# Reading the first batch's tokens in long stretches, fetching weights earlier, and moving the cluster copies to another DMA queue

## The chip, the cores and the metric

The kernel runs on one core of a Trainium2 chip. The metric is device time in microseconds (us) from launch to end; three runs of the kernel before gave 1026.86, 1027.94 and 1029.68, so the median is 1027.94. The profile is of one further execution, which took 1027.27 by the same clock and spans 1025.3 from its first to its last instruction. Sums made from the profile are sums against 1025.3.

## The reference

Two blocks are joined. The first is attention with routing: four batches, eight heads, 768 tokens, 64 numbers per head. Every token's query and key are assigned to the nearest of 16 centroids of the head, and a query only attends to keys of its own cluster. The second is a feed-forward block over all 3072 tokens, with a leaky slope per hidden unit.

```python
q_assign = np.argmax(np.einsum('bhsd,hcd->bhsc', q_n, c_n), axis=-1)
k_assign = np.argmax(np.einsum('bhsd,hcd->bhsc', k_n, c_n), axis=-1)
mask = q_assign[:, :, :, None] == k_assign[:, :, None, :]
scores = np.where(mask, scale * np.matmul(q, k.transpose(0, 1, 3, 2)), -1000000000.0)
attn = softmax(scores)
x = np.matmul(attn, v)             # then (B,H,S,D) -> (B*S, H*D)
h = x @ w_in                       # 512 -> 2048
out = (np.maximum(h, 0.0) + alpha * np.minimum(h, 0.0)) @ w_out   # 2048 -> 512
```

q, k, v and the centroids arrive as float32. The two weight matrices come as 64-bit floats, which the kernel reads as pairs of 32-bit words and turns into float32 itself, 128 by 512 numbers at a time.

## The kernel before, in words

**Steps.** Heads are handled two at a time: a pair `n` is a batch and two heads, 16 pairs in all. A pair's 768 queries are split in two halves of 384. The unit of the schedule is a step `u`: two of the six chunks of 128 keys, for one half of one pair, so three steps make a half. `steps` orders them: all four pairs of batch 0 with half 0 (u = 0 to 11), the same four with half 1 (u = 12 to 23), then batch 1, and so on, 96 steps. As soon as one half of a batch has gone through attention, its feed-forward work is cut into pieces (`ffn_pieces`, lines L611 on) that are spread over the next twelve steps. So u = 0 to 11 have attention alone on TensorE, and every later step has attention and feed-forward work.

**One step.** TensorE computes the scores (L467), for batch 0 it adds a mask product (L477) whose operands are `member` (which cluster a key is in) and `aq` (the same for queries), ScalarE takes the exponential (L488) into `E`, and one step later TensorE weighs the values with `E` (L577). In u = 0 to 11 it also sums the denominators, L570, into one fixed PSUM bank, `first_den`. When a half is done, VectorE turns and inverts the denominators (L583 to L596) and multiplies into `xT` (L604), which the feed-forward block reads (L627).

**Before a pair.** `load` and `load_v` bring q, k and v. For the first batch (`n < NCH`, NCH = 4) tokens lie 128 apart within a partition, so each DMA is cut into pieces of 64 floats, 256 bytes. `prep_features` transposes q and k on TensorE (L325), and ScalarE copies them to `qkT` (L329). `prep_sims` multiplies with the centroids (L352) into PSUM tile `mps`, of which there is one buffer, and `prep_argmax` takes the nearest centroid on VectorE (L360 to L382, seven instructions). `of_heads` (L386, ScalarE) makes the two heads' key masks, and `prep_queries` copies query rows to other partitions with two small DMAs (L427).

**Weights.** `convert` takes one block of 128 by 512 through stages: fetch (DMA, L238), split (VectorE, L241 and L243), scale (ScalarE, L247 and L249), join (VectorE, L253 and L256, then a multiplication on GpSimd, L259). 32 blocks are needed, half of w_in and half of w_out alternating in groups of four. There are five buffers `raw` for the fetched words and three `power`. Fetch is the first stage, so a block's DMA stands two slots ahead of its split in the order of the program; the scale follows four slots after the split and the join two after that.

**Order.** No scheduler is at work: the program's order is written out by hand. Each step has five slots, `later(k, piece)` puts a piece k slots on, and `prep_at` and `load_at` hold what is due at a step. Every engine runs its own instructions in that order. All DMAs but two small ones are issued by SP, in one queue, in program order too: a DMA that waits for a buffer or for an engine holds back those behind it.

```python
load_at.setdefault(max(u - 7, -AHEAD), []).append(
    lambda n=n: n < 2 or (load(n), load_v(n)))
at(u - (3 if n < NCH else 6), FIRST, lambda n=n: prep_sims(n))
at(u - 1, FIRST + h, lambda n=n, half=half, h=h: prep_queries(n, half, h))
converting = 0 if u < 1 else 1 + (u % 3 == 2) if u < UB else 2
```

The last line gives the conversions begun in a step: none at u = 0, 15 by the end of u = 11, two per step from u = 12 (UB) until all 32 are begun.

Of the kernel before, what the change touches and what calls it, by code (L numbers as in the profile page):

```python
# [9 lines left out]
FP32 = mybir.dt.float32  # L10
# [11 lines left out]
def kernel(  # L22
# [67 lines left out]
    def later(slots, piece):  # L90
        due.setdefault(now[0] + slots, []).append(piece)
# [13 lines left out]
    def load(n):  # L105


        b, hp = pairs[n]
        for w, src in enumerate((q, k)):
            raw = inp.tile([P, NJ, 2, D], FP32, name="qk")  # L110
            for h in range(2):
                rows = src[b, 2 * hp + h]
                if n < NCH:
                    nc.sync.dma_start(out=raw[:, :, h, :],
                                      in_=rows.rearrange("(j p) d -> p j d", p=P))
                    continue
                for x in range(D // Q):
                    r = h * D + x * Q
                    nc.sync.dma_start(  # L119
                        out=raw.rearrange("p j h d -> p (j h d)")[r:r + Q, :].rearrange(  # L120
                            "p (t i) -> p t i", i=Q),
                        in_=rows[:, x * Q:(x + 1) * Q].rearrange("(t p) i -> p t i", p=Q))
            raw_qk[n, w] = raw

    def load_v(n):
        b, hp = pairs[n]
        vt = vpool.tile([P, 2, NJ, D], FP32, name="vt")
        nc.sync.dma_start(
            out=vt.rearrange("p h j d -> p (h j) d"),
            in_=v[b, 2 * hp:2 * hp + 2].rearrange("h (j p) d -> p (h j) d", p=P))  # L130
        vts[n] = vt
# [4 lines left out]
    nc.scalar.dma_start(out=alf, in_=moe_alpha.rearrange("(f p) -> f p", p=P))  # L136
    for n in range(2):
        load(n)
        load_v(n)

# [90 lines left out]
    def convert(src, dst):  # L231
        raw = raw_tiles[0]
        raw_tiles.append(raw_tiles.pop(0))
        lo, hi = raw[:, :, 0], raw[:, :, 1]
        power = cvt.tile([P, CW], U32, name="power")

        def fetch():
            nc.sync.dma_start(out=raw.rearrange("p n w -> p (n w)"), in_=src)  # L238

        def split():  # L240
            nc.vector.tensor_scalar(out=power, in0=hi, scalar1=0x7FF00000, scalar2=None,  # L241
                                    op0=ALU.bitwise_and)
            nc.vector.tensor_scalar(out=dst.bitcast(U32), in0=hi, scalar1=0x000FFFFF,  # L243
                                    scalar2=None, op0=ALU.bitwise_and)

        def scale():
            nc.scalar.activation(out=power, in_=power, func=AF.Relu,  # L247
                                 bias=low_exp[:, 0:1], scale=8.0)
            nc.scalar.activation(out=dst, in_=dst.bitcast(U32), func=AF.Identity,  # L249
                                 bias=1.0, scale=2.0 ** -20)  # L250

        def join():
            nc.vector.scalar_tensor_tensor(  # L253
                out=power, in0=hi, scalar=0x80000000, in1=power,
                op0=ALU.bitwise_and, op1=ALU.bitwise_or)
            nc.vector.scalar_tensor_tensor(  # L256
                out=dst, in0=lo, scalar=2.0 ** -52, in1=dst,
                op0=ALU.mult, op1=ALU.add)
            nc.gpsimd.tensor_tensor(out=dst, in0=dst, in1=power.bitcast(FP32),  # L259
                                    op=ALU.mult)  # L260
        return [fetch, split, scale, join]


# [6 lines left out]
    for f0 in range(0, NF, FQ):  # L270
# [4 lines left out]
                    for f in range(f0, f0 + FQ)]  # L275
    under_way = deque()
    converted = [0]

# [8 lines left out]
    def convert_next():  # L287
        if sources:
            under_way.append(convert(*sources.popleft()))
            advance(under_way[-1])  # L290
# [28 lines left out]
    def prep_features(n, g):  # L319
        if n not in qkTs:  # L320
            qkTs[n] = qkp.tile([P, NB * P], FP32, name="qkT")
        ps = misc()
        for i, t in enumerate(groups[g]):
            w, j = divmod(t, NJ)
            nc.tensor.transpose(out=ps[:, i * P:(i + 1) * P],  # L325
                                in_=raw_qk[n, w][:, j].rearrange("p h d -> p (h d)"),
                                identity=ident)
        t0, m = groups[g][0], len(groups[g])
        later(1, lambda: nc.scalar.copy(qkTs[n][:, t0 * P:(t0 + m) * P],  # L329
                                        ps[:, 0:m * P]))  # L330

    def prep_blocks(n, w):
        if w == 0:
            qkTs[n] = qkp.tile([P, NB * P], FP32, name="qkT")
        nc.vector.transpose(out=qkTs[n][:, w * S:(w + 1) * S],
                            in_=raw_qk[n, w].rearrange("p j h d -> p (j h d)"))

# [20 lines left out]
    def prep_argmax(n, ps):  # L358
# [31 lines left out]
        members[n] = member  # L390
        later(4, of_heads)

# [25 lines left out]
    def prep_queries(n, half, h):  # L418

        if h == 0:  # L420
            aqs[n, half] = aqp.tile([P, 2, HS], BF16, name="aq")
        if n < NCH:

            if h == 0:
                r = slice(half * Q, (half + 1) * Q)
                for g in range(NG // 2, NG):
                    nc.sync.dma_start(out=aqs[n, half][g * Q:(g + 1) * Q, 0, :],  # L427
                                      in_=members[n][r, 0, :])
            return
        own_half = everys[n].rearrange("p g i r h -> p g (i r) h")[:, half, :, h:h + 1]  # L430
        nc.vector.transpose(out=aqs[n, half][:, h, :],
                            in_=own_half.broadcast_to((P, NX, Q)))
# [178 lines left out]
    def ffn_pieces(b, half):  # L611
        xT = xTs[b, half]
        rows = out[b * S:(b + 1) * S, :].rearrange("(j p) n -> p j n", p=P)
        gs, pss, ys, negs = {}, {}, {}, deque()
# [69 lines left out]
    for (n, half), u in start_of.items():  # L684
        def at(step, slot, piece):
            prep_at.setdefault((step, slot), []).append(piece)
        if half == 0:
            if n < NCH:
                load_at.setdefault(max(u - 7, -AHEAD), []).append(
                    lambda n=n: n < 2 or (load(n), load_v(n)))  # L690
            else:
# [5 lines left out]
            else:  # L697
                for w in range(2):
                    at(u - 7, FIRST + w, lambda n=n, w=w: prep_blocks(n, w))
            at(u - (3 if n < NCH else 6), FIRST, lambda n=n: prep_sims(n))  # L700
            if n >= NCH:
# [19 lines left out]
    for u in range(-AHEAD, TOGETHER):  # L721
# [33 lines left out]
        take = (max(len(ffn) - KEEP - whole * (UB - 1 - u % UB) // UB, 0) if ffn else 0)  # L755
        converting = 0 if u < 1 else 1 + (u % 3 == 2) if u < UB else 2
        for i in range(SLOTS - FIRST):
# [5 lines left out]
            if i < converting:  # L763
                convert_next()
        if s == SB - 1 and u >= UB:
            total(n, half)
# [3 lines left out]
    for u in range(TOGETHER, NS + 1):  # L770
# [37 lines left out]
        for i in slots:  # L808
# [4 lines left out]
            left = UB // SB * FREE - 1 - at_slot  # L813
            pieces = len(ffn) - (NS - u <= UB) - whole * left // (UB // SB * FREE)
            todo.popleft()()
# [178 lines left out]
```

## Time and profile before

| what | us |
|---|---|
| median of three runs | 1027.94 |
| span of the profiled execution | 1025.3 |
| PE busy | 996.5 (97%) |
| DVE (VectorE) busy | 678.6 (66%) |
| ACT (ScalarE) busy | 325.5 (32%) |
| first score matmul of u = 0 starts | 17.68 |
| first matmul of the feed-forward block starts | 88.06 |
| first score matmul of u = 24 (second batch) starts | 213.88 |

The shares are means over stages that differ, so the table gives the times that separate the stages too. Up to 17.68 the kernel loads and prepares; from there to about 88 it runs u = 0 to 11; from there to 213.88 it runs u = 12 to 23; from 213.88 on, it runs the other three batches and the rest of the feed-forward work. A PE that is shown as busy can still be waiting inside a group of matmuls, and matmuls overlap, so stage times are read from starts, not from busy time.

### The profile page before, as it was taken

Reading aid. Unit: us, or ns where it says so; the run is one execution under the profiler, and the core shown is the slowest. Engines: PE = TensorE matmul, PEld = TensorE weight load, DVE = VectorE, ACT = ScalarE, POOL = GpSimd, SP = SyncE. Lnnn points to the kernel's source line nnn. Section 1 sums busy time; section 2 is a strip of 40 time slices with the busy share of each in tenths; the row PEclk is TensorE's granted clock in tenths of the full one; section 3 lists DMA queues with packets and bytes.
Section 4 is the critical chain, followed back from the end, with each engine's and each line's share of the span. In section 5 each row is a group of like instructions: output and inputs, shape, how many; then the busy total and the mean of one; then the engine's idle time right before and its main releaser. Section 6 shows DMA issues by size and latency. Waiting matters only on the chain.

```text
span 1025.3 us, 10333 instructions
## 1 busy us (share of the span) xinstructions
PE 996.5 (97%) x3923; PEld 489.3 (48%) x3923; DVE 678.6 (66%) x1183; ACT 325.5 (32%) x620; POOL 53.0 (5%) x71
## 2 busy tenths in 40 slices
PE   7889999899999999999999999999999999999997
PEld 4434444345454554545455454545445454544453
DVE  3797788788575675878756676878857675662111
ACT  3765544233132332313233241413324041321120
POOL 1223222100000000000000000000000000000000
PEclk8989999999999999999999999999999999999999
DMA  9433664020000232022000221313000000000000
GB/s 207 152 126 108 134 147 110 17 59 18 1 1 11 52 47 36 11 56 37 1 0 1 62 35 12 47 34 59 1 1 1 31 0 1 1 11 20 1 0 34
DMA packets 121705, 43.13 MB, mean 42 GB/s; under 512 B 113952, under 2 KB 114480, under 8 KB 121648
## 3 DMA queue, kind: packets, MB, share of 16 engines
q1 hardware_dynamic: 121472, 42.35, 19.0%
q8 instruction: 33, 0.54, 0.2%
q14 instruction: 24, 0.20, 0.1%
q10 hardware_dynamic: 176, 0.04, 0.0%
HBM read 35.69 MB, written 6.29 MB: 41 GB/s over the span
## 4 chain that ended last, share of the span: by engine, by line
PE 86%; DVE 9%; issue 1%; POOL 1%; DMA 1%; ACT 1%; SPq 1%; DVEq 0%; POOLq 0%
PE fps L627 31%; PE fps L647 30%; PE vps L577 10%; PE sps L467 8%; PE fps L467 3%; DVE power L253 1%; PE mps L352 1%; DVE w_in_sb L243 1%; DVE w_in_sb L256 1%; DVE power L241 1%; DVE w_out_sb L256 1%; DVE acc L512 1%; DVE w_out_sb L243 1%; POOL w_in_sb L259 0%; SPq L119 0%
## 5 line engine op out<-in xcount | busy, mean ns | idle before, releaser
L627 PE MATMUL fps<-xT,w_in_sb 128*128 128x384 f32 x1024 | 341.0, 490 | 1.1 <-DVE xT L604 1.1
L647 PE MATMUL fps<-w_out_sb,gT 128*128 128x512 f32 x768 | 335.6, 594 | 0.9 <-DVE gT L619 0.9
L627 PEld LDWEIGHTS fps<-xT,w_in_sb 128*128 128x128 f32 x1024 | 191.2, 190 | 145.0 <-issue 5.3
L647 PEld LDWEIGHTS fps<-w_out_sb,gT 128*128 128x128 f32 x768 | 144.7, 190 | 177.8 <-issue 167.4
L619 DVE SCALAR_TENSOR_TENSOR gT<-neg,alpha_neg,gT 128x384 f32<-128x384 f32 x128 | 78.3, 613 | 130.8 <-ACT neg L635 129.4
L634 ACT ACTIVATE gT<-fps 128x384 f32<-128x384 f32 x128 | 62.7, 490 | 273.8 <-PE fps L627 273.8
L467 PE MATMUL sps<-qkT 64*128 64x384 f32 x576 | 113.0, 512 | 0.0
L501 DVE SCALAR_TENSOR_TENSOR raw<-aq,key,raw 128x384 f32<-128x384 bf16 x160 | 88.7, 613 | 16.8 <-ACT raw L485 10.9
L488 ACT ACTIVATE E<-sps 128x768 f32<-128x768 f32 x88 | 67.1, 812 | 68.4 <-PE sps L477 42.3
L577 PE MATMUL vps<-E,vt 128*64 128x384 f32 x448 | 83.3, 500 | 1.0 <-DVE xT L604 1.0
L501 DVE SCALAR_TENSOR_TENSOR E<-aq,key,E 128x384 f32<-128x384 bf16 x128 | 71.2, 612 | 10.5 <-ACT E L485 5.5
L467 PEld LDWEIGHTS sps<-qkT 64*128 64x128 f32 x576 | 52.9, 191 | 42.3 <-issue 9.3
L512 DVE TENSOR_TENSOR acc<-acc,E 128x768 f32<-128x768 f32 x64 | 66.4, 1038 | 8.2 <-ACT E L488 6.4
L655 DVE TENSOR_TENSOR y<-y,fps 128x512 f32<-128x512 f32 x30 | 20.5, 684 | 67.0 <-PE fps L647 67.0
L635 ACT ACTIVATE neg<-fps 128x384 f32<-128x384 f32 x128 | 62.1, 485 | 0.0
L488 ACT ACTIVATE raw<-sps 128x768 f32<-128x768 f32 x56 | 42.9, 814 | 52.6 <-PE sps L467 51.9
L577 PE MATMUL vps<-raw,vt 128*64 128x384 f32 x320 | 56.5, 491 | 0.0
L653 ACT COPY y<-fps 128x512 f32<-128x512 f32 x24 | 14.1, 585 | 130.0 <-PE fps L647 130.0
L577 PEld LDWEIGHTS vps<-E,vt 128*64 128x64 f32 x448 | 29.6, 138 | 42.5 <-issue 40.5
L512 DVE TENSOR_TENSOR acc<-acc,raw 128x768 f32<-128x768 f32 x48 | 45.9, 956 | 1.1
L467 PE MATMUL fps<-qkT 64*128 64x384 f32 x192 | 41.4, 508 | 0.0
L485 ACT ACTIVATE raw<-fps 128x384 f32<-128x384 f32 x48 | 21.0, 494 | 59.2 <-PE fps L467 59.2
(98 smaller groups left out, 617.8 us busy)
## 6 DMA issues: line engine op xcount, KB each, us to landing
raw<-in_moe_w_in_dram SPq DMA_DIRECT2D x16, 512.0 KB, 4.4
raw<-in_moe_w_out_dram SPq DMA_DIRECT2D x16, 512.0 KB, 3.7
vt<-in_v_dram SPq DMA_DIRECT2D x16, 384.0 KB, 4.3
out_dram<-y SPq DMA_DIRECT2D x24, 256.0 KB, 2.0
qk<-in_q_dram SPq DMA_DIRECT2D x48, 96.0 KB, 4.1
qk<-in_k_dram SPq DMA_DIRECT2D x48, 96.0 KB, 3.6
qk<-in_q_dram SPq DMA_DIRECT2D x8, 192.0 KB, 4.5
qk<-in_k_dram SPq DMA_DIRECT2D x8, 192.0 KB, 4.5
```

Source lines behind the costliest of these rows:

```text
L243: nc.vector.tensor_scalar(out=dst.bitcast(U32), in0=hi, scalar1=0x000FFFFF, scalar2=None, op0=ALU.bitwise_and)
L467: nc.tensor.matmul(out=bank(ps, h), lhsT=qkT[r:r + D, S + c * P:S + (c + 1) * P], rhs=qkT[r:r + D, half * HS:(half + 1) * HS], start=True, ...
L485: nc.scalar.activation(out=E[:, h, :], in_=ps[h][:, 0:HS], func=AF.Exp, scale=SCALE)
L488: nc.scalar.activation(out=E, in_=ps[:, :, 0:HS], func=AF.Exp, scale=SCALE)
L501: nc.vector.scalar_tensor_tensor(out=E[:, h, :], in0=aqs[n, half][:, h, :], scalar=keys[n][:, NJ + c, h:h + 1], in1=E[:, h, :], op0=ALU.is ...
L512: nc.vector.tensor_tensor(out=acc, in0=acc if first is None else first[3], in1=E, op=ALU.add)
L577: nc.tensor.matmul(out=po[r:r + D, 0:HS], lhsT=vts[n][:, h, c, :], rhs=e[:, h, :], start=(c == 0), stop=(c == NJ - 1))
L619: nc.vector.scalar_tensor_tensor(out=gs[f], in0=neg, scalar=alpha_neg[:, f:f + 1], in1=gs[f], op0=ALU.mult, op1=ALU.add)
L627: nc.tensor.matmul(out=ps[:, 0:HS], lhsT=w_in_sb[:, c, f * P:(f + 1) * P], rhs=xT[:, c, :], start=(c == 0), stop=(c == NCH - 1))
L634: nc.scalar.activation(out=gs[f], in_=ps[:, 0:HS], func=AF.Relu)
L635: nc.scalar.activation(out=neg, in_=ps[:, 0:HS], func=AF.Relu, scale=-1.0)
L647: nc.tensor.matmul(out=ps[:, 0:DM], lhsT=gs[f][:, i * P:(i + 1) * P], rhs=w_out_sb[:, f, :], start=on and f == f0, stop=off and f == f0 + ...
```

## The change

1. **Layout of the first batch.** In `load`, q and k of a pair `n < 4` are read with one DMA each (before: one per head), and a partition gets six neighbouring tokens, so a contiguous piece is 6 x 64 floats, 1536 bytes. `load_v` does the same. The tile `raw` is [P, 2, NJ, D]. As a head's 64 columns are now apart from the other's, each 128 x 128 transpose becomes two plain matmuls with the identity, one per head, each writing 64 partitions. The rows of `out` for batch 0 follow the same order of tokens.
2. **Order of loads.** At the start only q, k, v of pair 0 and q, k of pair 1 are loaded; v of pair 1 and the pairs 2 and 3 come at u = 0 to 3.
3. **Weights.** The DMA of a conversion is no longer its first stage: `fetch` issues up to three blocks ahead (two from u = 12), from u = -1 on. Conversions begin at u = 0: two each at u = 0 and 1, then 1 + (u % 4 == 3), which makes 17 by the end of u = 11 instead of 15.
4. **Cluster copies.** The two copies for the first half of pair 0 become VectorE copies; the other copies for batch 0 are DMAs issued by ScalarE instead of SP.
5. **`of_heads`** comes 12 slots after the argmax for pair 0 and 7 for the others (before: 4).
6. **`prep_sims`** of the pairs that begin at u = 24 and 27 moves from u = 18 and 21 to u = 19 and 22.
7. A rounding: from u = 24 on, the number of feed-forward pieces taken in a slot is rounded the other way.

```diff
     def load(n):
         b, hp = pairs[n]
         for w, src in enumerate((q, k)):
-            raw = inp.tile([P, NJ, 2, D], FP32, name="qk")
+            raw = inp.tile([P, 2, NJ, D], FP32, name="qk")
+            if n < NCH:
+                nc.sync.dma_start(
+                    out=raw.rearrange("p h j d -> p h (j d)"),
+                    in_=src[b, 2 * hp:2 * hp + 2].rearrange("h (p j) d -> p h (j d)",
+                                                            j=NJ))
             for h in range(2):
                 rows = src[b, 2 * hp + h]
-                if n < NCH:
-                    nc.sync.dma_start(out=raw[:, :, h, :],
-                                      in_=rows.rearrange("(j p) d -> p j d", p=P))
-                    continue
...
-    for n in range(2):
-        load(n)
-        load_v(n)
+    load(0)
+    load_v(0)
+    load(1)
...
     def convert(src, dst):
         raw = raw_tiles[0]
         raw_tiles.append(raw_tiles.pop(0))
+        nc.sync.dma_start(out=raw.rearrange("p n w -> p (n w)"), in_=src)
...
-        return [fetch, split, scale, join]
+        return [split, scale, join]
...
+    def fetch(ahead):
+        while (sources and len(fetched) < ahead
+               and begun[0] + len(fetched) - converted[0] < len(raw_tiles)):
+            fetched.append(convert(*sources.popleft()))
...
         for i, t in enumerate(groups[g]):
             w, j = divmod(t, NJ)
-            nc.tensor.transpose(out=ps[:, i * P:(i + 1) * P],
-                                in_=raw_qk[n, w][:, j].rearrange("p h d -> p (h d)"),
-                                identity=ident)
+            for h in range(2):
+                nc.tensor.matmul(out=ps[h * D:(h + 1) * D, i * P:(i + 1) * P],
+                                 lhsT=raw_qk[n, w][:, h, j, :], rhs=ident,
+                                 start=True, stop=True)
...
-        later(4, of_heads)
+        later(12 if n == 0 else 7, of_heads)
...
                 for g in range(NG // 2, NG):
-                    nc.sync.dma_start(out=aqs[n, half][g * Q:(g + 1) * Q, 0, :],
-                                      in_=members[n][r, 0, :])
+                    to = aqs[n, half][g * Q:(g + 1) * Q, 0, :]
+                    if n == 0 and half == 0:
+                        nc.vector.tensor_copy(out=to, in_=members[n][r, 0, :])
+                    else:
+                        nc.scalar.dma_start(out=to, in_=members[n][r, 0, :])
...
-                load_at.setdefault(max(u - 7, -AHEAD), []).append(
-                    lambda n=n: n < 2 or (load(n), load_v(n)))
+                if n > 1:
+                    load_at.setdefault(max(u - 7, 0), []).append(lambda n=n: load(n))
+                if n > 0:
+                    load_at.setdefault(max(u - 6, 0), []).append(lambda n=n: load_v(n))
...
-            at(u - (3 if n < NCH else 6), FIRST, lambda n=n: prep_sims(n))
+            at(u - (3 if n < NCH else 5 if u - 6 < TOGETHER else 6), FIRST,
+               lambda n=n: prep_sims(n))
...
-        converting = 0 if u < 1 else 1 + (u % 3 == 2) if u < UB else 2
+        converting = 0 if u < 0 else 2 if u < 2 else 1 + (u % 4 == 3) if u < UB else 2
...
+            if u >= -1:
+                fetch(3 if u < UB else 2)
...
-            pieces = len(ffn) - (NS - u <= UB) - whole * left // (UB // SB * FREE)
+            pieces = len(ffn) - (NS - u <= UB) + -whole * left // (UB // SB * FREE)
```

## The prediction

> **What bounds the kernel now.** I read the busy shares first, then a table by stage, then the waits, the chain and the timeline. The busy shares show TensorE at 97%, which leaves little to win on average. The table by stage says where the little is. Its columns are the stretch, its length, then busy time (and instructions) of PE, PEld, DVE, ACT and POOL, the granted clock, the DMA share and GB/s.
>
> ```profile
> PE 996.5 (97%) x3923; PEld 489.3 (48%) x3923; DVE 678.6 (66%) x1183; ACT 325.5 (32%) x620; POOL 53.0 (5%) x71
> ...
> 0.00:17.75 17.75, 10.46 (x59) 7.74 (x59) 5.92 (x19) 6.99 (x11) 4.74 (x39) 0.94 1.16 197
> 17.75:22.76 5.01, 5.01 (x22) 1.60 (x24) 0.00 (x1) 1.95 (x3) 0.00 (x0) 0.53 1.11 245
> 22.76:91.33 68.57, 61.06 (x478) 25.75 (x479) 60.39 (x120) 41.15 (x63) 19.25 (x13) 0.93 0.46 143
> 91.33:213.88 122.55, 116.42 (x454) 53.11 (x454) 97.14 (x164) 54.34 (x97) 28.96 (x19) 1.00 0.42 91
> 213.88:1025.30 811.42, 803.50 (x2915) 401.09 (x2914) 515.17 (x882) 221.03 (x447) 0.00 (x0) 1.00 0.11 22
> ```
>
> The last 811 us are TensorE alone, and nothing in the change shortens them. From 22.76 to 91.33 DVE is busy for 60.39 of 68.57 us, and TensorE's count hides waits: a step there has 8 score matmuls (1.56), 4 mask products (0.50), 16 denominator matmuls (0.86) and 8 weighing matmuls (1.51), and undisturbed steps start 4.15 apart (22.61 and 26.76). Eleven steps of 4.15, two transposed pairs of 1.9 and two centroid products of 0.8 make 51, against 66.2 from u = 0 (17.68) to u = 12 (83.91). The waits of DVE and PE show the gaps (waiting, for what: total, times, longest):
>
> ```profile
> DVE simT L360 <- PE mps L352: 8.3, 1, 8.3
> DVE power L241 <- DMA raw<-in_moe_w_in_dram: 5.0, 1, 5.0
> ...
> PE mps L352 <- DVE inv L544: 3.8, 2, 2.9
> PE mps L534 <- DVE part L524: 1.4, 2, 0.9
> PE fps L627 <- DVE xT L604: 1.1, 1, 1.1
> ```
>
> So DVE sits idle for 8.3 before 22.76 and 5.0 before 32.35, and from there works through a backlog until `xT` of pair 3 lets the feed-forward block go on at 91.33. Later the two centroid products at u = 18 and 21 hold PE for 3.8. The timeline shows the three mechanisms:
>
> ```profile
> 14.54 1.43 ACT L386 ACTIVATE member<-member,pick 64x384 bf16<-64x384 bf16 x2 [5.86 <-DVE member L382]
> 14.81 2.32 SPq L427 DMA_DIRECT2D aq<-member  x2
> 15.99 0.58 ACT L329 COPY qkT<-fps 128x512 f32<-128x512 f32 x1
> ...
> 20.54 0.82 PE L477 MATMUL sps<-aq,member 32*128 32x384 bf16 x4
> ...
> 27.93 1.53 SPq L238 DMA_DIRECT2D raw<-in_moe_w_in_dram  x3
> ...
> 34.40 1.39 POOL L259 TENSOR_TENSOR w_in_sb<-w_in_sb,power 128x512 f32<-128x512 f32 x1 [28.36 <-DVE w_in_sb L256]
> 34.56 1.51 DVE L243 TENSOR_SCALAR w_in_sb<-raw 128x512 uint32<-128x512 uint32 x1
> ```
>
> ScalarE's copies of pair 1 (15.99) stand behind `member`, so the first scores start late and on a slow clock (0.53). SP brings the next three weight blocks only at 27.93, behind a cluster copy that waits. And a DVE operation beside GpSimd's multiplication takes 1.51 instead of 0.42.
>
> **What the skill says.** SBUF — State Buffer, "Who interferes with whom": DVE and GpSimd share a port pair as an exclusive lock, and the one that starts second waits for the whole instruction. The trace agrees: L243 0.42 against 1.48 to 1.51, L256 0.68 against 1.77. So each conversion costs DVE about 1.08 more than its own work. DMA: Bandwidth & Descriptors, "Specifications", puts the smallest transfer at full rate at 512 bytes. The trace agrees in direction: 197 GB/s at a share of 1.16 where 256-byte pieces dominate, 143 at 0.46 where weights do. The same page, "Issuing engines are not separate DMA queues": another issuing engine saves only time on the sequencer; no row of before shows both. TensorEngine Tiling (Array Packing), "Restrictions and Gotchas", excludes fp32 transpose mode from column tiling, while "Key Properties" lets tiles run in parallel; L577 (64 columns) starts every 0.168 (4.02 for 24) where L627 (128 columns, same length) needs 0.327, so that agrees.
>
> **The change, part by part.**
>
> *Start.* The two-matmul transposes: 12 of 0.128 per pair (0.66 for four, less latency) become 48 instructions. From L577's 0.168 for 384 columns, 128 columns take 0.056, so 2.7; if each weight load (0.134, L212) were exposed, 6.4. I take 2.9, that is 1.4 more per pair. For pair 0 the wait for k (0.36 + 0.56) partly goes, so the copies end 0.9 later. The centroid product ends at 11.4 instead of 10.5, and the seven argmax operations (3.9) at 15.4. Then come two DVE copies (a bound of 0.17 from L593 and 0.58 from L382; I take 0.3 each, in place of 2.32 of issue plus landing) beside two L386 (1.43): masks are ready at 16.9. Pair 1's copies no longer stand behind L386, so its transposes and the scores of u = 0 are through by about 15.5. The mask product starts at 16.9 instead of 20.54. With 0.5 for it and 0.9 for the centroid product of pair 1, DVE's second argmax starts at 18.4 instead of 22.76: **4.4 earlier**.
>
> *DVE from there to `xT` of pair 3.* Before: 15 splits of 0.67 (10.0), 13 joins of 1.20 (15.6), 13 port stalls of 1.08 (14.0), 3 argmax of 3.87 (11.6), 4 normalisations of 2.9 (11.5); 62.7, plus the 5.0 for the DMA, is 67.7 of the real 68.4 (22.76 to 91.2). So the sum holds. After, the order of DVE has 17 splits and 15 joins before that point, the first split already done: 16 x 0.67 + 15 x 2.28 + 11.6 + 11.5 = 68.0, and 0.8 for small waits. 18.4 + 68.8 = 87.2, against 91.2: **4.0 earlier**, and two conversions (5.9) are done beyond that. The wait of 5.0 goes because blocks 0 to 2 are issued right behind k of pair 1, with nothing to wait for. Whether they arrive: 1.97 MB of q, k, v and 0.52 of block 0 from about 2 at 197 GB/s land near 15, needed at 16. Block 3 has 5.6 MB up to its end and is needed near 25: 250 GB/s suffices. At the old 197 it is 5 late; at 143/0.46 = 311 (an estimate from the table) it is 5 early. I take no wait. PE has some 15 us of slack here, which hides the dearer transposes of pairs 2 and 3 (2.8) and late cluster copies at u = 3 to 12.
>
> *From 91.33 to 213.88.* FFN work decides: the 122.55 holds some 114 of PE work. The centroid products move one step later, when `mps` has long been read: 3.8 go. Their results are needed by L399 in the step after: 12.9 after the start of u = 19 (3.4 + 0.8 + 5.4 + 3.4), against VectorE's end near 12 (exponentials at 4.3, two sums 2.9, split and join 1.9, argmax 2.6); nothing lost, at worst 1. With 15 conversions left instead of 17, the second wait for `part` (0.9) mostly goes. **4.3 earlier**, bounds 2 and 7.
>
> *Queues.* ScalarE issues 14 of the 16 copies: 1.15 per two (L427), on an engine busy 54.34 of 122.55. SP is rid of them. Each copy stands behind the exponentials and scales of its step, and the lane it waits for was used several DMAs earlier. For u = 15: exponentials and two scales end by 111.5, issue 1.2, median landing 3.4, so 116.1, against 118.93 when L477 starts. It is in time by 2.8; at the longest landing seen (6.1) barely. I take nothing. The rounding (7) reorders work in a saturated stretch: nothing. `of_heads` later: ScalarE's rest hides it. The rows of `out` stay 2048 bytes: nothing.
>
> *Sum.* 4.0 + 4.3 is 8.3; I keep 8 for reordering. 1025.3 - 8 = 1017.3. The profiled run was timed at 1027.27 and the median is 1027.94, so 1027.94 - 8 = **1019.9**.
>
> **Rivals.** A change within 3.1 us (0.3%) is not told from none here.
>
> *A, the forecast:* both gains. Chance 0.58, range 1016 to 1023.5.
>
> *B, the head start is spent.* The two extra conversions and late weights eat it: block 3 lands 5 late, `xT` comes at about 92, and only the later gain of 2 to 4 remains: 1024 to 1026. For it: DMA is at a share of 1.16 up to 17.75, and three weight blocks now stand before v of pair 1. Against: 1536-byte pieces. 0.2.
>
> *C, more.* DVE's two conversions also free the waits for power buffers (L241, 1.38 each) at u = 12 to 20, and the full 5.9 turns into PE time: 8.3 + 4 gives 1015.5. For it: the chain runs through DVE from 145.8 to 187. Against: PE is at 95% there. 0.1.
>
> *D, slower.* ScalarE's queue: a copy's landing becomes the last thing L477 waits for at u = 15, 18, 21, and the exponentials behind a DMA issue wait with it. It decides once the issue moves over 2.8 late. To eat 8 and lose 3.5 it must cost 3.8 at each of three places, so landings near 10 us, or a lane held by a weight block waiting on DVE. Then 1031.5. Against: longest landing 6.1. 0.08.
>
> *E, the change doesn't do what it says:* VectorE is behind anyhow and everything ends where it did: 1027. 0.04.
>
> **Numbers.** Faster by over 0.3% (under 1024.9): all of A and C, half of B: 0.78. Same: half of B, and E: 0.14. Slower: D, 0.08. The range for 8 in 10 takes A with both bounds of the second stage, most of B and the middle of C: 1014 to 1026.5.
>
> **What would show it.** Right: the first mask product near 17, the second argmax near 18.4, no wait of DVE for `raw`, 15 multiplications on GpSimd before `xT` of pair 3 near 87, no wait of L352 on `inv`, u = 24 near 205.6. Wrong: ScalarE or L477 waiting for `aq`, VectorE waiting for `raw`, or PE waits of another name between 87 and 206; and a changed length after u = 24, which I have at 811.4 on both sides.

## The result, and the profile after

The changed kernel takes 1021.83 us (median of 4 runs, 1020.31 to 1022.26), the kernel before 1027.4 beside it: a ratio of 0.9944, 95% interval 0.9917 to 0.9972, so it is faster by 5.6 us. The forecast was 1019.9. The direction was right and the likeliest value 1.9 too low. The stages show why: those before u = 24 gained a little more than forecast, and the one after it lost 3.2 where nothing was to change. The granted clock of TensorE differs too: of the 36 runs of the kernel before that stood beside the first variants below, those at a mean granted clock of 0.987 took 1029.6 in the median, those at 0.990 took 1026.5 and those at 0.994 took 1024.6, while the four runs of the changed kernel have 0.996 to 0.999. How much of the 5.6 comes with the clock was not separated.

The page of the changed kernel begins with the busy shares, and the table by stage has the same columns as before. Its borders are the second argmax, about the end of `xT` of pair 3 and the first scores of u = 24.

```profile
PE 998.6 (98%) x4067; PEld 491.3 (48%) x4067; DVE 671.5 (66%) x1185; ACT 325.0 (32%) x620; POOL 50.4 (5%) x71
...
0.00:17.80 17.80, 14.45 (x151) 10.89 (x151) 7.19 (x23) 8.69 (x14) 4.74 (x39) 1.00 0.91 323
17.80:87.67 69.87, 62.44 (x549) 28.62 (x550) 57.73 (x126) 45.70 (x71) 21.57 (x15) 0.95 0.44 140
87.67:204.96 117.29, 116.21 (x458) 53.54 (x456) 91.22 (x157) 49.79 (x90) 24.08 (x17) 1.00 0.43 86
204.96:1019.60 814.64, 805.55 (x2915) 398.27 (x2914) 515.38 (x882) 220.80 (x447) 0.00 (x0) 1.00 0.11 21
```

The reader is to compare lengths, not busy times. The second argmax starts 4.96 earlier than before (22.76). The next stretch is 1.3 longer, but holds 15 of GpSimd's multiplications instead of 13. The third is 5.3 shorter (122.55 before; from the start of `xT` in both, it is 117.8 instead of 123.3, so 5.5) and TensorE fills it all but 1.1 us. The last has the same number of matmuls and is 3.2 **longer** (811.42 before).

The waits of VectorE between 14 and 92, and of TensorE after 205 (waiting, for what: total, times, longest), read:

```profile
DVE simT L600 <- PE fps L587: 4.5, 3, 4.0
DVE power L246 <- POOL w_in_sb L264: 2.8, 2, 1.4
DVE power L258 <- ACT power L252: 1.8, 2, 1.0
DVE simT L374 <- PE mps L366: 1.7, 1, 1.7
DVE power L246 <- POOL w_out_sb L264: 1.2, 1, 1.2
...
PE mps L551 <- DVE part L541: 1.8, 2, 0.9
PE mps L855 <- DVE good L852: 1.2, 1, 1.2
PE mps L551 <- ACT every L417: 1.0, 1, 1.0
```

VectorE's 8.3 for the centroid product has become 1.7, and its 5.0 for `raw` is gone. New or longer are the other waits in the list, 10.3 in all, where the kernel before had 1.4. And after 205, TensorE waits twice 0.91 for `part`, in a stretch that the change touches only by a rounding and, for the rest of batch 0, by the order of the rows of `out`.

### The profile page after: what moved, and what is told of

Its sections match the earlier page's. It is cut to its first block, busy times and chain, and to the rows that moved or that the text cites. A ratio compares the mean times of both kernels' runs of the same rounds, so it can differ in the third digit from the quotient of the medians.

```text
span 1019.6 us, 10615 instructions
## 1 busy us (share of the span) xinstructions
PE 998.6 (98%) x4067; PEld 491.3 (48%) x4067; DVE 671.5 (66%) x1185; ACT 325.0 (32%) x620; POOL 50.4 (5%) x71
## 4 chain that ended last, share of the span: by engine, by line
PE 91%; DVE 4%; ACT 2%; DMA 1%; issue 1%; POOL 0%; ACTq 0%; DVEq 0%; POOLq 0%
PE fps L665 32%; PE fps L645 32%; PE vps L594 11%; PE sps L484 9%; PE fps L484 4%; PE mps L366 1%; PE sps L494 1%; ACT E L505 1%; ACT member L400 1%; DMA aq<-member 1%; PE mps L551 0%; ACT power L252 0%; PE fps L339 0%; PE fps L587 0%; DVE gT L637 0%
## 5 line engine op out<-in xcount | busy, mean ns | idle before, releaser
L637 DVE SCALAR_TENSOR_TENSOR gT<-neg,alpha_neg,gT 128x384 f32<-128x384 f32 x128 | 80.6, 636 | 100.2 <-ACT neg L653 99.5
L484 PE MATMUL sps<-qkT 64*128 64x384 f32 x576 | 110.9, 504 | 0.7 <-ACT E L505 0.7
L529 DVE TENSOR_TENSOR acc<-acc,E 128x768 f32<-128x768 f32 x64 | 61.2, 956 | 17.1 <-ACT E L505 15.3
```

Source lines behind the costliest of these rows:

```text
L484: nc.tensor.matmul(out=bank(ps, h), lhsT=qkT[r:r + D, S + c * P:S + (c + 1) * P], rhs=qkT[r:r + D, half * HS:(half + 1) * HS], start=True, ...
L529: nc.vector.tensor_tensor(out=acc, in0=acc if first is None else first[3], in1=E, op=ALU.add)
L637: nc.vector.scalar_tensor_tensor(out=gs[f], in0=neg, scalar=alpha_neg[:, f:f + 1], in1=gs[f], op0=ALU.mult, op1=ALU.add)
```

## Experiments

Each comparison is with the kernel before on the same chip; where two variants of the changed kernel are compared, both medians are given. L numbers of the changed kernel are meant, unless said.

### Where 3 us go after u = 24: the rounding

*The old rounding put back in the changed kernel.*

```diff
-            pieces = len(ffn) - (NS - u <= UB) + -whole * left // (UB // SB * FREE)
+            pieces = len(ffn) - (NS - u <= UB) - whole * left // (UB // SB * FREE)
```

> The changed kernel with the old rounding of the feed-forward pieces (floor of what may stay, instead of its ceiling). Theory R: the new rounding puts one feed-forward piece between the second-last work of a half and the next scores, and the switch of the array's tiling right ahead of the scores is then exposed, 0.09 to 0.1 us in each of about 24 halves, 2.3 to 2.5 in all. So 1021.8 becomes about 1019.4, u = 24 stays near 205.0, and what follows it shrinks from 814.6 to near 812. Rival: the 3.2 us lost after u = 24 are spread over the run or come from the other edits; then the time stays within 0.5 of the changed kernel, near 1021.8, and the stretch after u = 24 stays at 814 to 815.

Measured: 1017.37 (1017.15 to 1018.14, 5 runs), ratio to before 0.9901, interval 0.9882 to 0.992. `xT` of pair 3 and u = 24 stay where they were (87.18 and 204.96); after u = 24 it takes 810.5 instead of 814.6 (stretch, length, then the columns of the table above):

```profile
204.96:1015.50 810.54, 803.50 (x2915) 401.10 (x2914) 515.17 (x882) 221.01 (x447) 0.00 (x0) 1.00 0.11 22
```

So the rounding costs more than this expectation said: 4.1 in the profiled runs.

*The new rounding alone, in the kernel before* (the same line, exchanged the other way).

> The kernel before with the new rounding alone. Theory R: 2.4 us slower than before, 1029.8 to 1030.3, all of it after u = 24 in equal steps of 0.09 to 0.1 per half. Rival (rounding costs nothing, as predicted): within 0.5 of before, near 1027.5.

Measured: 1029.97 (22 runs), ratio 1.0032, interval 1.0021 to 1.0042: slower by 2.2 to 4.3 us, with 815.3 after u = 24 against 811.4.

```profile
211.46:1026.80 815.34, 805.55 (x2915) 399.00 (x2914) 515.31 (x882) 220.80 (x447) 0.00 (x0) 1.00 0.11 21
```

The change of order needs nothing else of the change to do its harm.

What does it do? The timelines at one end of a half (start, duration, line, matmuls) show it, here of the kernel before

```profile
424.44 0.30 PE L534 MATMUL mps<-part,fold 128*128 128x24 f32 x2
424.67 1.56 PE L467 MATMUL sps<-qkT 64*128 64x384 f32 x8
```

and of the changed one, TensorE and then its weight loads:

```profile
411.72 2.83 PE L645 MATMUL fps<-xT,w_in_sb 128*128 128x384 f32 x8
414.38 0.30 PE L551 MATMUL mps<-part,fold 128*128 128x24 f32 x2
414.52 2.83 PE L645 MATMUL fps<-xT,w_in_sb 128*128 128x384 f32 x8
417.28 1.56 PE L484 MATMUL sps<-qkT 64*128 64x384 f32 x8
...
417.28 0.95 PEld L484 LDWEIGHTS sps<-qkT 64*128 64x128 f32 x8 [0.55 <-issue]
```

A feed-forward piece now stands behind `total` (L551). Twice, then, a weight load isn't hidden: once behind the short matmuls of `total`, once at the scores, whose load starts only with the scores themselves although it had nothing to wait for. In the kernel before, both fall on the same spot. Sixteen feed-forward matmuls and `total` take 5.56 here (411.72 to 417.28). The Trainium skill, TensorEngine Tiling (Array Packing), "Key Properties", says that changing the tiling mode drains TensorE; the trace agrees in so far as the load for the 64-row scores doesn't run ahead, as those of the feed-forward block do. That a drain is the reason is not tested. The other half of the cost is that a piece *behind* `total` is missing *ahead* of it, and twice TensorE waits for VectorE's sums there:

```profile
293.39 0.40 PE L551 MATMUL mps<-part,fold 128*128 128x24 f32 x2 [0.91 <-DVE part L541]
```

To test this and not the rounding as such, the new rounding was kept and only the last slot of a half turned round.

```diff
-            todo.popleft()()
-            feed(max(pieces, 0))
+            if (s, i) == (SB - 1, SLOTS - 1):
+                feed(max(pieces, 0))
+                todo.popleft()()
+            else:
+                todo.popleft()()
+                feed(max(pieces, 0))
```

> The changed kernel, new rounding kept, with one swap: in the last slot of a half the feed-forward piece is issued ahead of the fold of the partial sums (total) and no longer between it and the scores. If the new rounding costs 4 us because of where its pieces stand (0.09 us more exposed weight loading in each of about 24 halves, 2.2; and two waits of 0.91 for part, 1.8), this gives nearly all of it back: 810 to 811 after u = 24, 1017.4 to 1018. If the cost comes from the other places where the rounding moves pieces to, it stays: 814 to 815 after u = 24, near 1021.8.

Measured: 1016.38 (1016.11 to 1016.93, 5 runs), ratio 0.9889, interval 0.9872 to 0.9906; 809.4 after u = 24. The same place now reads:

```profile
413.69 0.30 PE L551 MATMUL mps<-part,fold 128*128 128x24 f32 x2
413.92 1.56 PE L484 MATMUL sps<-qkT 64*128 64x384 f32 x8
```

The sixteen matmuls and `total` take 5.47 (408.45 to 413.92), 0.09 less. The difference to the kernel before, measured from u = 24 on, rises steadily by 0.089 per half in the changed kernel (1.27 at the fifth half, 2.70 at the 21st), and stays level here (-1.35 at both). No wait for `part` or `every` is left; the one for `every`, 1.0, stands in the kernel before too, so the swap gains somewhat more than the rounding had cost. So the rounding's cost is shown, and so is the place: 24 x 0.09 = 2.2 for the exposed loads (the step of 0.09 was read over sixteen halves and taken for all 24) and 2 x 0.91 = 1.8 for `part`, 4.0 against the 4.1 measured.

### What gained before u = 24

*`of_heads` at its old place.*

```diff
-        later(12 if n == 0 else 7, of_heads)
+        later(4, of_heads)
```

> The changed kernel with the per-head copies of the membership (of_heads) put in ScalarE's queue 4 ticks after the argmax as before, instead of 12 or 7. Prediction's step: the copies of pair 1's transposes then stand behind 1.43 us of of_heads again; the first mask product stays at 16.3 or comes earlier, the second argmax 1.4 later, near 19.2 to 19.9, and the same 1.4 or less remains in the time: 1022 to 1023.4. Rival: in the changed order the copies are long done, and nothing changes: within 0.5 of 1022.

Measured: 1025.61 (13 runs), against 1021.98 for the changed kernel; ratio to before 0.9981, interval 0.9969 to 0.9994. Neither expectation holds: the cost is 3.6, not 1.4. The timeline of this kernel, ScalarE, TensorE and VectorE:

```profile
15.19 1.43 ACT L400 ACTIVATE member<-member,pick 64x384 bf16<-64x384 bf16 x2 [5.70 <-DVE member L396]
16.65 0.59 ACT L343 COPY qkT<-fps 128x512 f32<-128x512 f32 x1
...
17.29 1.97 PE L339 MATMUL fps<-ident,qk 128*64 128x128 f32 x16 [4.24 <-ACT qkT L343]
...
23.87 0.58 DVE L374 STREAM_TRANSPOSE simT<-mps 128x384 f32<-128x384 f32 x1 [7.34 <-PE mps L366]
```

And the same of the changed kernel:

```profile
14.82 1.43 ACT L400 ACTIVATE member<-member,pick 64x384 bf16<-64x384 bf16 x2 [1.51 <-DVE member L396]
...
16.31 0.50 PE L494 MATMUL sps<-aq,member 32*128 32x384 bf16 x4 [1.23 <-ACT member L400]
...
17.80 0.58 DVE L374 STREAM_TRANSPOSE simT<-mps 128x384 f32<-128x384 f32 x1 [1.65 <-PE mps L366]
```

Price the wait, not the instruction. The two L400 take 1.43, but ScalarE, in order, stands for 5.70 ahead of them, and behind it is the copy that frees the PSUM tile for TensorE's third group of transposes, which waits 4.24. The scores of u = 0 and the second argmax come behind that.

They also come at a slower clock. TensorE's granted clock is 0.50 from 16.31 to 23.14 in this run, as it is from 15.60 to 22.43 in the kernel before; in the changed kernel it is 1.00 over both stretches. The first scores show it, in the kernel before, in this variant and in the changed kernel:

```profile
17.68 2.93 PE L467 MATMUL sps<-qkT 64*128 64x384 f32 x8
19.19 2.93 PE L484 MATMUL sps<-qkT 64*128 64x384 f32 x8
13.52 1.56 PE L484 MATMUL sps<-qkT 64*128 64x384 f32 x8
```

With the sixteen transposes (1.97 against 1.08) and the mask product (0.82 against 0.50), about 2.6 of the 6.07 by which the argmax is later than in the changed kernel is the clock, an estimate from these lengths. No run holds the clock fixed, so the order and the clock are not told apart further. With `of_heads` moved back, the argmax (23.87) is later than in the kernel before (22.76): without this line nothing is left of the head start of 5 us. Whether the line would bring it alone, without the two VectorE copies, was not run. This profiled run, at 1027.68, is among the longest of its variant; 3.6, from the medians, is the better figure for the cost.

*The centroid products one step later, alone, in the kernel before.*

```diff
-            at(u - (3 if n < NCH else 6), FIRST, lambda n=n: prep_sims(n))
+            at(u - (3 if n < NCH else 5 if u - 6 < TOGETHER else 6), FIRST,
+               lambda n=n: prep_sims(n))
```

> The kernel before with the centroid products of the pairs that need it moved one step later, alone. The prediction's step: the waits of 3.8 us on inv at u = 18 and 21 go, and nothing else changes: 1027.5 becomes 1023.5 to 1024, with xT of pair 3 still at 91. Rival: TensorE's wait is only moved, because the feed-forward block waits for VectorE elsewhere in the same stretch: a gain under 1.5 us, 1026 or more.

Measured: 1024.23 (12 runs), ratio 0.997, interval 0.9959 to 0.998: 2 to 4 us faster. From `xT` of pair 3 to u = 24 it is 120.8 instead of 123.3. The wait on `inv` is gone, and the waits of TensorE (lines of the kernel before) show what takes back a part of its 3.8:

```profile
PE fps L627 <- DVE y L655: 1.8, 1, 1.8
PE mps L534 <- DVE part L524: 1.1, 2, 0.6
PE fps L647 <- DVE gT L619: 0.9, 1, 0.9
```

The changed kernel needs 117.8 there, so 3.0 come from something else. In none of the variants of the changed kernel below are they lost (117.5 to 117.8 in each). What no run undid is that `fetch` is no longer a stage of a conversion, so that each later stage of it comes two slots earlier. The wait of 1.8 for `y` and that of 1.1 for `part` are the ones missing in the changed kernel; that the stages are the cause was only argued, and stays open.

### The edits in the title

The changed kernel was run again as a control for three of the variants.

> The changed kernel once more, as the control beside which the next three stand: 1021.8 as in its first runs, within 0.7; xT of pair 3 at 87.2, u = 24 at 205.0, 814.6 after it. If its time lies at 1023.7 in some runs, as with the copies in SyncE's queue, those 2 us are not due to the queue.

Measured: 1021.98 (1021.45 to 1022.35, 6 runs), ratio 0.9941, interval 0.9926 to 0.9957; `xT` of pair 3 at 86.61, u = 24 at 204.38, 814.9 after it.

*Pieces of 256 bytes for q, k and v, two-matmul transposes kept.*

```diff
             if n < NCH:
-                nc.sync.dma_start(
-                    out=raw.rearrange("p h j d -> p h (j d)"),
-                    in_=src[b, 2 * hp:2 * hp + 2].rearrange("h (p j) d -> p h (j d)",
-                                                            j=NJ))
+                for h in range(2):
+                    nc.sync.dma_start(out=raw[:, h],
+                                      in_=src[b, 2 * hp + h].rearrange("(j p) d -> p j d", p=P))
...
```

> The changed kernel with q, k and v of the first batch read in pieces of 256 bytes as before (the two-matmul transposes stay). If the long pieces matter by their rate (246 GB/s in the first slice against 207), q and k of pair 0 are 0.8 later, the weight blocks behind them 2 to 5 later: second argmax near 18.6 to 20, a wait of VectorE for raw of 1 to 5, xT of pair 3 at 88 to 92, time 1023 to 1027. Rival: the transfers are hidden anyway once the weights don't stand behind the cluster copies: second argmax within 0.8 of 18, no wait for raw over 0.5, time within 0.8 of 1022.

Measured: 1021.55 (1021.15 to 1022.11, 5 runs), ratio 0.9936, interval 0.9921 to 0.9952. The tables by stage of the variant, and then of the control, up to 17.75:

```profile
0.00:17.75 17.75, 14.51 (x147) 11.60 (x149) 7.18 (x23) 8.14 (x13) 4.74 (x39) 1.00 1.03 234
```

```profile
0.00:17.75 17.75, 14.51 (x145) 11.66 (x149) 7.18 (x23) 8.07 (x13) 4.75 (x39) 1.00 0.91 331
```

The long pieces do move more, 331 GB/s against 234. Nothing waits for it: the second argmax starts at 18.43 with short pieces and 18.51 with long ones, and VectorE doesn't wait for `raw` in either. The rival is right; the long pieces are worth nothing here. What the two-matmul transposes cost, which the new layout brought with it, was not run.

*One block fetched ahead.*

```diff
-                fetch(3 if u < UB else 2)
+                fetch(1)
```

> The changed kernel with one weight block fetched ahead of its conversion instead of three (two later). Prediction's step: the fetch ahead is what takes away VectorE's wait of 5.0 for raw; with only one ahead a wait of 1 to 3 us for raw comes back at the second and third conversions and xT of pair 3 lands at 89 to 91, u = 24 at 207 to 209, the time at 1024 to 1026. Rival: what matters is that fetches no longer stand behind the cluster copies in SyncE's queue, and one ahead is enough: no wait for raw over 0.5, xT of pair 3 within 0.7 of 87.2, time within 0.7 of 1021.8.

Measured: 1021.81 (6 runs), ratio 0.9938, interval 0.9922 to 0.9953; no wait for `raw`, 117.8 from `xT` to u = 24. The rival is right that one block ahead is enough. Its reason, that fetches no longer stand behind the cluster copies, isn't shown: with the copies back in that queue and three blocks ahead (next) VectorE doesn't wait for `raw` either, and the two together were not run.

*The cluster copies in SyncE's queue.*

```diff
-                        nc.scalar.dma_start(out=to, in_=members[n][r, 0, :])
+                        nc.sync.dma_start(out=to, in_=members[n][r, 0, :])
```

> The changed kernel with the cluster copies back in SyncE's queue (the two copies on VectorE stay). If the move to ScalarE's queue costs or gains nothing, as predicted, 1021.3 to 1022.3. If ScalarE's issues of about 0.6 us each and the wait of 1.69 for aq at u = 9 cost something, up to 1.5 us faster, 1020.3. If SyncE's queue is what held the copies up before (the issues there stand behind weight blocks that wait for their buffers), slower, 1023 to 1026.

Measured: 1023.69 (1021.51 to 1025.51, 9 runs), ratio 0.9956, interval 0.9941 to 0.9971, which overlaps the changed kernel's. Four of the nine runs lie at 1021.5 to 1021.8 and five between 1023.7 and 1025.5; none of the ten of the changed kernel is above 1022.4. The profiled run is one of the four, and shows about the same 87.52 for `xT` of pair 3 and 205.10 for u = 24, with TensorE waiting 3.8 for `aq` instead of 1.8, where VectorE sets the pace: `xT` of pair 3 is 0.36 later. ScalarE's queue thus seems to make the time steadier, by up to 1.9 us in the median. Not all variants ran on one chip; the one with the old rounding ran on the same chip as this one, with its copies in ScalarE's queue, and its five runs lie within 1.0. What happens in the other five runs was not profiled.

### The conversions begun early

```diff
-        converting = 0 if u < 0 else 2 if u < 2 else 1 + (u % 4 == 3) if u < UB else 2
+        converting = 0 if u < 1 else 1 + (u % 3 == 2) if u < UB else 2
```

> The changed kernel with the conversions spread over the steps as before (none at u = 0, 15 instead of 17 by u = 11). Theory of the prediction: the two early conversions use VectorE's idle time in front of the second argmax and are then missing from the stretch after xT of pair 3. Without them xT of pair 3 comes 2 to 4 us earlier (84 to 85), but the stretch from there to u = 24 grows by as much or more: u = 24 at 205 to 208, time 1022 to 1025. Rival: the schedule is worth nothing either way, since VectorE has room after 92: u = 24 at 202 to 203, and the time 1019 to 1020.

Measured: 1018.72 (1018.05 to 1019.83, 6 runs), ratio 0.9912, interval 0.9896 to 0.9928, 3.3 faster than the control. `xT` of pair 3 starts here at

```profile
83.94 0.56 DVE L621 TENSOR_TENSOR xT<-vps,rd 128x384 f32<-128x384 f32 x1
```

against 86.61 to 87.16 in the changed kernel, and the stretch from there to u = 24 is 117.5, not longer than the 117.8 with two conversions fewer. So neither expectation is quite right on the times, but the rival is on the mechanism: doing two conversions early costs 2 to 3 us where VectorE is the limit and saves none where TensorE is.

Not all of the 3.3 need be the conversions themselves. The profiled run of this variant has the full clock from the second argmax to u = 24, and four of its six runs a mean of 0.999 or 1.0, against 0.996 or 0.997 in nine of the ten of the changed kernel. Its two runs at 0.997 and 0.998 took 1019.8, about 2 under the control. Whether the edit is what keeps the clock up was not tested.

What a short fall of the clock costs can be read in the variants that leave the conversions as they are. In the changed kernel, VectorE's longest wait in this stage, for the denominators, follows 3.41 us (48.94 to 52.36) at a granted clock of 0.50; the control has the full clock there. The changed kernel, then the control:

```profile
54.22 0.38 DVE L600 STREAM_TRANSPOSE simT<-fps 128x192 f32<-128x192 f32 x1 [3.97 <-PE fps L587]
53.27 0.38 DVE L600 STREAM_TRANSPOSE simT<-fps 128x192 f32<-128x192 f32 x1 [2.50 <-PE fps L587]
```

From the second argmax to the start of `xT` of pair 3 it is 69.36, 69.38 and 69.36 in the three profiled kernels with such a stretch near 50 (the changed one, the old rounding, one block ahead), and 68.10, 67.86 and 68.06 in the three without (the control, the last slot turned round, the short pieces). All six have another one at about 68 to 71.

### A version that beats both

*The two edits that gained, together.* The diffs are those of the last-slot swap and of the conversions.

> The changed kernel with the conversions spread as before (15 by u = 11) and the fold of the partial sums issued after the last piece of its half: the two edits that gained, together. If they are independent: 1021.98 - 3.26 - 5.60 = 1013.1; xT of pair 3 at 84, u = 24 at 201.5, 809.4 after it. If the early conversions, too, only shifted pieces between halves, the gains overlap and it stays at 1015 to 1016.

Measured: 1013.44 (1013.19 to 1014.12), ratio 0.9858, interval 0.984 to 0.9875: 13.9 us less than the kernel before, 8.5 less than the control. u = 24 is at 202.15, with 809.4 after it; the gains add.

*In this version, the multiplication on VectorE.*

```diff
-            nc.gpsimd.tensor_tensor(out=dst, in0=dst, in1=power[0].bitcast(FP32),
+            nc.vector.tensor_tensor(out=dst, in0=dst, in1=power[0].bitcast(FP32),
```

> The same kernel, with the last multiplication of each conversion on VectorE instead of GpSimd. The prediction's price: each conversion stalls VectorE 1.08 beside GpSimd's multiplication; on VectorE it costs about 0.65 (from the row y<-y,fps), so 0.43 less for each, and no wait of a split for GpSimd's result. 13 to 15 of them lie before xT of pair 3: 5.6 to 6.4 earlier at most, 78 instead of 84, if TensorE doesn't become the limit first: then 80 to 82. Time 1008 to 1011. Rival: what looked like a stall is VectorE's own work, the multiplication adds its 0.65 to each and xT of pair 3 comes 8 to 10 us later, time near 1022.

Measured: 1017.36 (5 runs), ratio 0.9893, interval 0.9876 to 0.9909: 3.9 slower than on GpSimd. VectorE's groups between 17 and 84 (count, busy, mean ns), first on VectorE:

```profile
L246 DVE TENSOR_SCALAR power<-raw 128x512 uint32<-128x512 uint32 x14 | 5.9, 418 | 0.0
L264 DVE TENSOR_TENSOR w_in_sb<-w_in_sb,power 128x512 f32<-128x512 f32 x8 | 5.5, 692 | 0.3
...
L248 DVE TENSOR_SCALAR w_in_sb<-raw 128x512 uint32<-128x512 uint32 x8 | 3.4, 421 | 0.0
L248 DVE TENSOR_SCALAR w_out_sb<-raw 128x512 uint32<-128x512 uint32 x6 | 2.5, 422 | 0.0
```

and then on GpSimd:

```profile
L246 DVE TENSOR_SCALAR power<-raw 128x512 uint32<-128x512 uint32 x15 | 8.4, 558 | 2.4 <-POOL w_in_sb L264 2.4
L248 DVE TENSOR_SCALAR w_in_sb<-raw 128x512 uint32<-128x512 uint32 x8 | 7.7, 960 | 0.0
L248 DVE TENSOR_SCALAR w_out_sb<-raw 128x512 uint32<-128x512 uint32 x7 | 6.2, 883 | 0.0
```

The stall is real: without GpSimd all these operations fall to 0.42, as the Trainium skill (SBUF — State Buffer, "Who interferes with whom") has it for a port pair that two engines share. But it is smaller than the prediction's price: (8.4 + 7.7 + 6.2) less 15 x 0.84 is 9.7, over 13 multiplications 0.75 each, where VectorE's own multiplication takes 0.69. There is nothing to gain. Why 3.9 are lost isn't settled: VectorE waits 8.8 for the denominators on TensorE (2.3 on GpSimd) and the granted clock is 0.92 instead of 1.00 between 17.75 and 84; either can be a result as well as a cause.

## Why the prediction was right or wrong

**Start: right, and for the reason given.** Forecast and profiled run: first mask product 16.9 and 16.31, second argmax 18.4 and 17.80 (18.51 in the control), transposes 2.9 per pair and 3.2 and 2.9, the two VectorE copies 0.3 each and 0.27. That pair 1's copies no longer stand behind `of_heads` was named; the experiment shows that nothing of the head start is left without it. One part was not argued: the prediction read the slow clock of the first scores (0.53) and then reckoned with the lengths at the full one (0.5 and 0.9). The clock did stay up, which was luck as far as the working goes. In *Queues* the prediction called the later `of_heads` hidden by ScalarE's rest, which is true of it and hides that it is, of the lines that a run took back, the most valuable of the change.

**VectorE to `xT` of pair 3: the total was right, its terms were not.** 87.2 was forecast, 87.7 measured. But the stall of 1.08 per conversion, 16.2 for 15, was too much. By the same subtraction as above, VectorE's own two-input operations included, it was about 6.8 in the changed kernel (1.0 at L246, 3.3 at L248, 2.5 at L258 and L261), and 12.7 for 13 in the kernel before, where the price had been read. Why it fell is open. In its place came the waits listed above, 10.3 instead of 0.8. Two errors of nearly 10 us cancel, and that the sum came out is luck. Of the 10.3, some 1.3 belongs to the clock of the profiled run: the control, without the fall near 50, takes 68.1 where that run takes 69.4. That no wait for `raw` is left was right; the rate that the prediction worked out for it didn't matter.

**Two conversions done beyond that: their cost was in the sum, their return was not there.** The forecast expected the second wait for `part` (0.9) to go because of them, and rival C more. The stretch that was to be shorter has the same length without them, so that they only cost: 3.3 us in the medians, about 2 where the clock is alike.

**From 91 to 214: right in size, 5.3 against 4.3 (bounds 2 and 7), partly for another reason.** Of the 5.5 from the start of `xT`, the centroid products alone gave 2.5 in the profiled run, not 3.8, since the waits moved to `y` and `part`; 3.0 came from what is still open. u = 24 begins at 204.96, forecast 205.6.

**Queues: the copies' move is within what was forecast** (nothing), rival D didn't come: they were never late by more than 1.7, and the move gains if anything (steadier times).

**The step that failed is "the rounding (7) reorders work in a saturated stretch: nothing"**, and with it "811.4 on both sides". It costs 4.1 (810.5 against 814.6). A saturated stretch hides other engines' work behind TensorE, but not TensorE's own order: with TensorE busy for 805.55 of 814.64 us, the exposed weight load is paid in full 24 times and the wait for `part` twice. The prediction had named a changed length after u = 24 as what would prove it wrong, and that is where it was. Against the 811.4 of the kernel before, 3.2 of it appear in the changed kernel's trace. With that term 1019.9 becomes 1023.1; of the 1.3 that the time came out lower, 0.9 are the stages before u = 24, which gained 8.9 in the profiled runs and not 8, and the remaining 0.4 is covered by the kernel before, which stood at 1027.4 and not 1027.94 beside it.

**The rivals.** B's head start was not spent, C's extra gain didn't come, D and E didn't occur: A it was, less the rounding, which neither A nor any rival contained.

## What to carry to other kernels

In a stretch that one engine fills, the order on that engine is what is left to pay for: look at what stands directly ahead of every change of matmul shape, and cost a reordering by its count, not by its kind. Price an in-order queue's instruction by what it waits for and who stands behind it: 1.43 us of work with a wait of 5.70 ahead of it cost 3.6 us of the whole. Read the granted clock of a stage beside its lengths before explaining a difference by the order alone. Work done early is only worth something if the stage that it leaves is limited by the same engine; here it was moved from one that TensorE limits to one that VectorE limits.

## What the runs showed of the hardware that was not expected

- A weight load for a 64-row matmul behind a 128-row stream starts only with the matmul. Together with `total` standing apart it costs 0.09 us each time, and it repeats to 0.01 from half to half in every profiled kernel that has the new order, the changed one and the kernel before with the rounding alone among them.
- Reading 1536-byte pieces instead of 256-byte ones took the rate in the first 17.75 us from 234 to 331 GB/s, without any effect on the time.
- VectorE's stall beside GpSimd's multiplication is not one price: a mean of 0.98 per conversion in the kernel before (12.7 over 13), 0.75 in the best version, about 0.45 (6.8 over 15) in the changed one.
- The granted clock of TensorE fell to 0.50 for 3.41 or 6.83 us at a time. One such stretch of 3.41 near 50 us made the way from the second argmax to `xT` of pair 3 about 1.3 longer (three profiled kernels at 69.4 against three at 67.9 to 68.1), through VectorE's wait for the denominators.
